# Linear attention in one pass: first q ahead of first v, filling matmuls behind the second head's transposes, v in whole rows for four of six buffers

## The chip, the cores and the metric

The kernel runs on one core of a Trainium2 chip. A core has TensorE (PE: matrix products, which take 128x128 weights, loaded by PEld, and stream columns past them), VectorE (DVE), ScalarE (ACT), GpSimd (POOL) and SyncE (SP), which here only issues transfers. PE writes to PSUM, eight banks of 512 fp32 columns on 128 partitions; everything else is kept in SBUF. Sixteen DMA engines move data between SBUF and the memory outside. The metric is the device time of one execution in microseconds (us).

## The reference

For each of 32 heads with 2048 rows of q, k and v, 128 wide, in bf16:

```python
phi_q = jnp.where(q > 0, q + 1, jnp.exp(q)) + 1e-6
phi_k = jnp.where(k > 0, k + 1, jnp.exp(k)) + 1e-6
kv  = jnp.einsum("bhsd,bhse->bhde", phi_k, v)      # 128 x 128 for each head
z   = jnp.einsum("bhsd->bhd", phi_k)               # sum of phi_k over the rows
num = jnp.einsum("bhqd,bhde->bhqe", phi_q, kv)
den = jnp.einsum("bhqd,bhd->bhq", phi_q, z)[..., None] + 1e-6
return num / den
```

The kernel writes phi(x) as min(exp(x), 1) + 1e-6 plus max(x, 0), and for most tiles never adds the two halves: PE accumulates both products.

## The kernel before, in words

A head is 16 tiles of 128 rows. Each head's q, k and v come in as one transfer of 512 KB, 4 KB on each partition, into one of six input buffers (NBI, head number modulo six, `bi`); results leave from ten output buffers.

For head h, in order of the data:

- ACT makes `ek_sb` = exp(k) (line 329); DVE turns it into `emk_sb` (min with 1, plus epsilon, line 335); POOL makes `rk_sb` = max(k, 0) (line 331) and, for tiles 1 to 5 (ADD), adds the two halves (line 340).
- PE multiplies phi(k) by v into the one bank `kvz_ps` (lines 356 and 359): two products for each of the eleven tiles of SPLIT, one for each of the five of ADD, 27 in all, which I call kv. The sum z needs a further column of ones beside v. Where a tile of v lies next to a gap of ones in SBUF, the product takes 129 columns at once. Everywhere else a matmul of a single column follows, with the same weights (`mm_held`, recorded under line 278).
- PE transposes q, 16 times, into `x_ps` (line 374); ACT makes exp of both halves (`eq_sb`, line 385) and max(q, 0) of the second (line 388), DVE that of the first (line 391); DVE makes `emq_sb` (line 394).
- ACT and DVE copy kv and z to `kvs_sb` (lines 364 and 366). PE multiplies phi(q) by it into the five banks `o_ps` (lines 412 and 418): the numerators and, as a 129th column, the denominators. DVE adds epsilon, takes reciprocals and multiplies (lines 457, 461, 433, 439). In the last heads ACT takes a part of that.

v lies in SBUF as two groups of eight tiles, with 32 columns of ones ahead of, between and behind them; one POOL memset of all three gaps in all six buffers makes these (line 274). So tiles 0, 7, 8 and 15 have ones at their side, and a row of v arrives as two pieces of 2 KB. Head 0 is another matter: its v goes to a buffer of its own, `v0_sb`, without gaps.

The order on each engine is a sort by a key given to every step (`Plan.add`), roughly the head's number plus a fraction; semaphore waits follow from what a step reads and writes. On PE a round is: numerators of head h, then transposes and kv of head h+2; ahead of the first round stand transposes and kv of heads 0 and 1. Heads in the middle are a loop of four turns of six heads on PE. On SP the stores have keys that grow faster than the heads', so that they fall behind the loads.

Until the first q is there, PE runs twelve products of zeros, 128x512 each, into the banks `o_ps` 2 to 4 (`warm`, lines 289 and 278, called on line 297). The first loads are issued in this order. On SP: k of head 0, q of head 0, k of head 1, q of head 1, v of head 1, and so on. On ACT's own queue: v of head 0 (line 316).

Of the kernel before, what the change touches and what calls it, by code (L numbers as in the profile page):

```python
# [11 lines left out]
def _ap(base: bass.AP, elem_offset: int, dims):  # L12
    return bass.AP(base.tensor, base.offset + elem_offset, [list(base.ap[0])] + [list(d) for d in dims])
# [162 lines left out]
def bass_standalone__linear_attn_elu__prompt_kernel(  # L176
# [6 lines left out]
    B, H, S, D = q.shape  # L183
    assert D == P and S == 16 * P
    NT = 16
# [3 lines left out]
    NBI = 6  # L189
# [6 lines left out]
    SPLIT = tuple(j for j in range(NT) if j not in ADD)  # L196
    GAP, GRP = 32, 8 * D
    VW = 2 * GRP + 3 * GAP

# [13 lines left out]
    LOOP, TURNS = 3, 4  # L215
# [6 lines left out]
    with ExitStack() as es:  # L222
# [4 lines left out]
        v_sb = sb("v_sb", [P, NBI, VW], bf16)  # L227
        q_sb = sb("q_sb", [P, NBI, NT * D], bf16)
        v0_sb = sb("v0_sb", [P, NT * D], bf16)
# [29 lines left out]
        pl = Plan()  # L259

        def rows(x, h):
            return x[h].rearrange("(p j) d -> p (j d)", j=NT)
# [8 lines left out]
        pl.add("pool", -7, lambda g: g.memset(ones_sb[:], 1.0), writes=[("ones",)])  # L271

        vfull = v_sb[:, :, :]
        pl.add("pool", -7, lambda g: g.memset(_ap(vfull, 0, [[VW, NBI], [GAP + GRP, 3], [1, GAP]]), 1.0), writes=[("vones",)])

        def mm_held(pe, out, lhsT, rhs, start, stop):

# [5 lines left out]
        def warm(n):  # L283

            def f(pe):
# [8 lines left out]

        pl.add("act", -9, lambda a: a.activation(rden_sb[:, 0, 0:1], warm_sb[:, 0:1], ACT.Exp), reads=[("warm",)],
               writes=[("rden", 0, 0)])
        pl.add("pe", -9, warm(12), reads=[("warm",)], writes=[("banko", 2), ("banko", 3), ("banko", 4)])

# [6 lines left out]
        for h in range(NH):  # L307
# [4 lines left out]

            def load(name, buf, src, key, h=h, bi=bi):
                dst, rws = buf[:, bi], rows(src, h)
                if h == 0 and name == "v":
                    pl.add("act", -8, lambda a: a.dma_start(v0_sb[:], rws), writes=[(name, bi)], dma=("x", 0))
                    return
                if name == "v":
                    dst = _ap(vfull, bi * VW + GAP, [[GAP + GRP, 2], [1, GRP]])
                    rws = rws.rearrange("p (a b) -> p a b", b=GRP)  # L320
                pl.add("sp", key, lambda sp: sp.dma_start(dst, rws), writes=[(name, bi)], dma=(name, bi))  # L321
# [22 lines left out]
            def kv(pe, tiles, srcs, h=h, bi=bi, b3=b3):  # L344
                for j in tiles:
                    for src in srcs:
                        first, fin = (j == SPLIT[0] and src is emk_sb), j == ADD[-1]
                        w = src[:, b3, j * D:(j + 1) * D]
                        c = GAP + (GAP + GRP) * (j // 8) + D * (j % 8)
                        l, r = (1, 0) if j % 8 == 0 else (0, 1) if j % 8 == 7 else (0, 0)  # L350
                        z = NC * r if h == 0 else 0
                        if h == 0:
                            rhs, l, r = v0_sb[:, j * D:(j + 1) * D], 0, 0
                        else:
                            rhs = v_sb[:, bi, c - l:c + D + r]
                        last = pe.matmul(kvz_ps[:, 1 - l:NC + r], lhsT=w, rhs=rhs, start=first, stop=fin,  # L356
                                         skip_group_check=True)
                        if not l + r:
                            last = mm_held(pe, kvz_ps[:, z:z + 1], w, ones_sb[:, 0:1], False, fin)
                return last  # L360
            pl.add("pe", at("kv", -1.2), lambda pe, kv=kv: kv(pe, SPLIT, (emk_sb, rk_sb)),
                   reads=[("emk", b3), ("rk", b3), ("v", bi), ("ones",), ("vones",)], writes=[("bankkv",)])
            pl.add("pe", at("kv", -1.2), lambda pe, kv=kv: kv(pe, ADD, (rk_sb,)), reads=[("phik", b3), ("v", bi)], writes=[("bankkv",)])
            pl.add("act", at("kvs", -0.95), lambda a, b3=b3: a.activation(kvs_sb[:, b3, 1:], kvz_ps[:, 1:NC], ACT.Copy),
                   reads=[("bankkv",)], writes=[("kvs", b3)])
# [123 lines left out]
            for n, (t0, t1) in enumerate(PIECES.get(h, ((0, NT),))):  # L489
                store(t0, t1, late + 0.01 * n, bo if n == 0 else NBO + EXTRA[h] + n - 1)  # L490

        pl.emit(block, sems, dma_sem, ("pe", 1 + LOOP * 9, NBI * 9, TURNS))


# [26 lines left out]
```

## Time and profile before

| What | us |
| --- | --- |
| median of three runs | 170.31 |
| lowest and highest of them | 170.14, 170.51 |
| the profiled execution | 170.35 |
| its span, first to last instruction | 168.5 |

| Engine | busy us | share of the span |
| --- | --- | --- |
| PE (matmuls) | 159.2 | 94% |
| PEld (loads of weights) | 151.7 | 90% |
| ACT | 158.1 | 94% |
| DVE | 150.3 | 89% |
| POOL | 105.5 | 63% |
| transfers of q1, the main queue | | 98.7% of 16 engines' span |

The profile is one execution. A group's busy time is the union of its instructions; matmuls overlap, so that a record of 0.22 us may be followed by the next one after 0.06 us: what a step costs on PE is read from start to start. The idle time before an instruction is shown with what ended it. The page's strips cut the span into 40 slices of 4.2 us, with a digit for tenths of the slice; PEclk is the granted clock of TensorE in the same tenths.

### The profile page before, as it was taken

The numbers are of one execution on the slowest core, as the hardware profiler recorded it, in microseconds if no ns is written. First come the engines' busy times: TensorE is split into PE (matmuls) and PEld (weight loads), VectorE is DVE, ScalarE is ACT, GpSimd is POOL, SyncE is SP. The second block draws the span as 40 slices with busy tenths as digits, with TensorE's granted clock in tenths as the row PEclk, the third lists the DMA queues.
The fourth block names the chain that finished last, engine by engine and source line by source line (L and its number), as shares of the span: only waits on it lengthen the run. The fifth ranks groups of instructions, "written<-read, shape, count | busy, mean of one in ns | idle before, by whom it ended". The sixth has DMA issues, their size and how long they took to land.

```text
span 168.5 us, 6577 instructions
## 1 busy us (share of the span) xinstructions
PE 159.2 (94%) x3092; PEld 151.7 (90%) x2401; DVE 150.3 (89%) x293; ACT 158.1 (94%) x180; POOL 105.5 (63%) x72
## 2 busy tenths in 40 slices
PE   7959999999999999999999999999999999999960
PEld 0459999999999999999999999999999999999940
DVE  0164799999999999999999999999999999999890
ACT  4699999999999999999999999999999999996980
POOL 3837746666777666666777666666777666666200
PEclk9995999999999999999999999999999999999997
DMA  5999999999999999999999999999999999999984
GB/s 207 408 415 410 411 409 407 409 406 414 412 408 410 416 415 415 419 414 416 415 415 416 417 410 420 414 419 415 415 414 417 418 414 417 413 413 416 391 327 163
DMA packets 22852, 67.33 MB, mean 400 GB/s; under 512 B 2100, under 2 KB 2612, under 8 KB 22836
## 3 DMA queue, kind: packets, MB, share of 16 engines
q1 hardware_dynamic: 22692, 66.59, 98.7%
q10 hardware_dynamic: 144, 0.52, 0.8%
q8 instruction: 10, 0.16, 0.4%
q14 instruction: 6, 0.05, 0.1%
HBM read 50.33 MB, written 16.78 MB: 398 GB/s over the span
## 4 chain that ended last, share of the span: by engine, by line
PE 88%; DMA 3%; DVE 3%; ACT 3%; issue 0%; SPq 0%
PE kvz_ps L356 36%; PE o_ps L412 32%; PE x_ps L374 16%; DMA q_sb<-in_q_dram 3%; DVE o_sb L439 1%; PE o_ps L278 1%; ACT eq_sb L385 1%; PE kvz_ps L278 1%; PE o_ps L418 1%; ACT ek_sb L329 1%; ACT rq_sb L388 1%; DVE emk_sb L335 0%; DVE rden_sb L461 0%; DVE den_sb L457 0%; SPq L321 0%
## 5 line engine op out<-in xcount | busy, mean ns | idle before, releaser
L340 POOL TENSOR_TENSOR rk_sb<-rk_sb,emk_sb 128x640 bf16<-128x640 bf16 x32 | 44.7, 1396 | 48.1 <-DVE emq_sb L394 43.8
L356 PE MATMUL kvz_ps<-v_sb,rk_sb 128*128 128x128 bf16 (+1 forms) x512 | 68.4, 219 | 0.0
L439 DVE TENSOR_TENSOR o_sb<-o_ps,rden_sb 128x768 bf16<-128x768 f32 (+2 forms) x63 | 68.0, 1119 | 0.1
L385 ACT ACTIVATE eq_sb<-x_ps 128x1024 bf16<-128x1024 bf16 x64 | 62.0, 1022 | 3.3 <-PE x_ps L374 3.3
L329 ACT ACTIVATE ek_sb<-k_sb 128x2048 bf16<-128x2048 bf16 x32 | 61.9, 1933 | 1.7 <-DMA k_sb<-in_k_dram 1.7
L331 POOL TENSOR_SCALAR rk_sb<-k_sb 128x2048 bf16<-128x2048 bf16 x32 | 60.6, 1894 | 2.7 <-DMA k_sb<-in_k_dram 2.0
L412 PE MATMUL o_ps<-kvs_sb,emq_sb 128*128 128x129 bf16 x474 | 60.7, 220 | 0.3 <-DVE o_sb L439 0.3
L412 PE MATMUL o_ps<-kvs_sb,rq_sb 128*128 128x129 bf16 x474 | 60.7, 220 | 0.0
L356 PE MATMUL kvz_ps<-v_sb,emk_sb 128*128 128x128 bf16 (+1 forms) x352 | 55.8, 220 | 2.1 <-DVE kvs_sb L366 2.1
L278 PE MATMUL kvz_ps<-ones_sb,rk_sb 128*128 128x1 bf16 x388 | 53.6, 167 | 0.0
L356 PEld LDWEIGHTS kvz_ps<-v_sb,rk_sb 128*128 128x128 bf16 x512 | 47.5, 98 | 1.5
L412 PEld LDWEIGHTS o_ps<-kvs_sb,rq_sb 128*128 128x128 bf16 x474 | 46.3, 98 | 0.0
L412 PEld LDWEIGHTS o_ps<-kvs_sb,emq_sb 128*128 128x128 bf16 x474 | 45.6, 98 | 0.6 <-DVE o_sb L439 0.4
L278 PE MATMUL kvz_ps<-ones_sb,emk_sb 128*128 128x1 bf16 x228 | 37.8, 167 | 0.0
L356 PEld LDWEIGHTS kvz_ps<-v_sb,emk_sb 128*128 128x128 bf16 x352 | 34.0, 98 | 2.3 <-issue 2.3
L374 PEld LDWEIGHTS x_ps<-ident,q_sb 128*128 128x128 bf16 x512 | 29.9, 98 | 5.5 <-DMA q_sb<-in_q_dram 5.5
L374 PE MATMUL x_ps<-ident,q_sb 128*128 128x128 bf16 x512 | 33.8, 219 | 0.3 <-DMA q_sb<-in_q_dram 0.3
L388 ACT ACTIVATE rq_sb<-x_ps 128x1024 bf16<-128x1024 bf16 x32 | 33.1, 1035 | 0.0
L335 DVE TENSOR_SCALAR emk_sb<-ek_sb 128x2048 bf16<-128x2048 bf16 x32 | 21.9, 684 | 8.3 <-ACT ek_sb L329 8.3
L391 DVE TENSOR_SCALAR rq_sb<-x_ps 128x1024 bf16<-128x1024 bf16 x32 | 21.8, 681 | 2.0 <-ACT eq_sb L385 2.0
L394 DVE TENSOR_SCALAR emq_sb<-eq_sb 128x2048 bf16<-128x2048 bf16 x32 | 22.7, 708 | 0.4 <-ACT eq_sb L385 0.4
L433 DVE TENSOR_TENSOR o_sb<-o_ps,rden_sb 128x128 bf16<-128x128 f32 x31 | 9.0, 291 | 1.0
(39 smaller groups left out, 80.2 us busy)
## 6 DMA issues: line engine op xcount, KB each, us to landing
k_sb<-in_k_dram SPq DMA_DIRECT2D x32, 512.0 KB, 13.2
q_sb<-in_q_dram SPq DMA_DIRECT2D x32, 512.0 KB, 13.1
v_sb<-in_v_dram SPq DMA_DIRECT2D x31, 512.0 KB, 13.6
out_dram<-o_sb SPq DMA_DIRECT2D x29, 512.0 KB, 13.4
out_dram<-o_sb SPq DMA_DIRECT2D x2, 320.0 KB, 9.2
out_dram<-o_sb SPq DMA_DIRECT2D x3, 192.0 KB, 3.6
v_sb<-in_v_dram ACTq DMA_DIRECT2D x1, 512.0 KB, 4.2
out_dram<-o_sb SPq DMA_DIRECT2D x1, 184.0 KB
```

The source lines that it names most:

```text
L278: return pe.add_instruction(mybir.InstMatmult(name=nc.get_next_instruction_name(), engine=mybir.EngineType.PE, ldweights=False, ins=[pe.lo ...
L329: lambda a, bi=bi, b2=b2: a.activation(ek_sb[:, b2, :], k_sb[:, bi, :], ACT.Exp),
L331: pl.add("pool", h, lambda g, bi=bi, b3=b3: g.tensor_scalar(rk_sb[:, b3, :], k_sb[:, bi, :], BIG, 0.0, op0=ALU.min, op1=ALU.max), reads=[( ...
L335: lambda d, b2=b2, b3=b3: d.tensor_scalar(emk_sb[:, b3, :], ek_sb[:, b2, :], 1.0, EPS, op0=ALU.min, op1=ALU.add),
L340: pl.add("pool", h + 0.5, lambda g, added=added: g.tensor_tensor(out=added(rk_sb), in0=added(rk_sb), in1=added(emk_sb), op=ALU.add), reads ...
L356: last = pe.matmul(kvz_ps[:, 1 - l:NC + r], lhsT=w, rhs=rhs, start=first, stop=fin, skip_group_check=True)
L374: last = pe.transpose(xT_ps[:, j * P:(j + 1) * P], q_sb[:, bi, j * P:(j + 1) * P], ident[:])
L385: lambda a, b2=b2, c=cols(half): a.activation(eq_sb[:, b2, c], xT_ps[:, c], ACT.Exp),
L388: lambda a, b3=b3, c=cols(1): a.activation(rq_sb[:, b3, c], xT_ps[:, c], ACT.Relu),
L394: lambda d, b2=b2, b3=b3: d.tensor_scalar(emq_sb[:, b3, :], eq_sb[:, b2, :], 1.0, EPS, op0=ALU.min, op1=ALU.add),
L412: last = pe.matmul(o_ap, lhsT=x[:, b3, t * P:(t + 1) * P], rhs=kvs_sb[:, b3, :], start=first, stop=not first)
L439: return lambda d: d.tensor_tensor(out=o_sb[:, bo, t0:t1, :].rearrange("p (a b) d -> p a b d", b=n), in0=_ap(nfull(b), 512 * b + NC * (t0 ...
```

## The change

There are three edits.

1. The first q is issued from ACT's queue, where the first v was. The first v takes the next key on SP, second there, behind the first k, and lands in `v0_sb` as before.
2. The warming products ahead of the first transposes are eleven, not twelve. Five more, of the same form, are placed on PE between the second head's transposes and its kv (key -0.22).
3. For buffers 1, 2, 4 and 5 (`WHOLE`) v lies as one group of sixteen tiles with ones ahead and behind, and its row arrives as one piece of 4 KB. There only tiles 0 and 15 have ones at their side; tiles 7 and 8 get the one-column matmul. Buffers 0 and 3 stay as they were. The ones are set by three POOL memsets. Of heads 1 to 31, 21 use a buffer with whole rows.

PE's loop begins one step later in its list, since there is one step more ahead of it.

```diff
+    WHOLE = (1, 2, 4, 5)
...
-        pl.add("pool", -7, lambda g: g.memset(_ap(vfull, 0, [[VW, NBI], [GAP + GRP, 3], [1, GAP]]), 1.0), writes=[("vones",)])
+        for n, (c, dims) in enumerate(((0, [[VW, NBI]]), (GAP + GRP, [[3 * VW, 2], [GAP + GRP, 2]]),
+                                       (VW + GAP + 2 * GRP, [[3 * VW, 2], [VW, 2]]))):
+            pl.add("pool", -7, lambda g, c=c, dims=dims: g.memset(_ap(vfull, c, dims + [[1, GAP]]), 1.0), writes=[("vones", n)])
...
-        pl.add("pe", -9, warm(12), reads=[("warm",)], writes=[("banko", 2), ("banko", 3), ("banko", 4)])
+        pl.add("pe", -9, warm(11), reads=[("warm",)], writes=[("banko", 2), ("banko", 3), ("banko", 4)])
+
+        pl.add("pe", -0.22, warm(5), reads=[("warm",)], writes=[("banko", 2), ("banko", 3), ("banko", 4)])
...
+                if h == 0 and name == "q":
+                    pl.add("act", -8, lambda a: a.dma_start(dst, rws), writes=[(name, bi)], dma=("x", 0))
+                    return
                 if h == 0 and name == "v":
-                    pl.add("act", -8, lambda a: a.dma_start(v0_sb[:], rws), writes=[(name, bi)], dma=("x", 0))
-                    return
-                if name == "v":
+                    dst = v0_sb[:]
+                elif name == "v" and bi in WHOLE:
+                    dst = v_sb[:, bi, GAP:GAP + 2 * GRP]
+                elif name == "v":
                     dst = _ap(vfull, bi * VW + GAP, [[GAP + GRP, 2], [1, GRP]])
                     rws = rws.rearrange("p (a b) -> p a b", b=GRP)
...
-                        c = GAP + (GAP + GRP) * (j // 8) + D * (j % 8)
-                        l, r = (1, 0) if j % 8 == 0 else (0, 1) if j % 8 == 7 else (0, 0)
+                        n = NT if bi in WHOLE else NT // 2
+                        c = GAP * (1 + j // n) + D * j
+                        l, r = (1, 0) if j % n == 0 else (0, 1) if j % n == n - 1 else (0, 0)
...
-        pl.emit(block, sems, dma_sem, ("pe", 1 + LOOP * 9, NBI * 9, TURNS))
+        pl.emit(block, sems, dma_sem, ("pe", 2 + LOOP * 9, NBI * 9, TURNS))
```

More of the change, by code (lines that the diff above doesn't have):

```diff
@@ L361, in bass_standalone__linear_attn_elu__prompt_kernel @@
             pl.add("pe", at("kv", -1.2), lambda pe, kv=kv: kv(pe, SPLIT, (emk_sb, rk_sb)),
-                   reads=[("emk", b3), ("rk", b3), ("v", bi), ("ones",), ("vones",)], writes=[("bankkv",)])
+                   reads=[("emk", b3), ("rk", b3), ("v", bi), ("ones",)] + [("vones", n) for n in range(3)],
+                   writes=[("bankkv",)])
             pl.add("pe", at("kv", -1.2), lambda pe, kv=kv: kv(pe, ADD, (rk_sb,)), reads=[("phik", b3), ("v", bi)], writes=[("bankkv",)])
```

## The prediction

> **What bounds the kernel now.** I read the page from the top: engines, clock and DMA over time, and the chain that ended last.
>
> ```profile
> PE 159.2 (94%) x3092; PEld 151.7 (90%) x2401; DVE 150.3 (89%) x293; ACT 158.1 (94%) x180; POOL 105.5 (63%) x72
> ...
> PEclk9995999999999999999999999999999999999997
> DMA  5999999999999999999999999999999999999984
> ...
> PE 88%; DMA 3%; DVE 3%; ACT 3%; issue 0%; SPq 0%
> ```
>
> Four resources look full: PE, ACT, DVE and the DMA engines. The chain says which of them the end hangs on: 88% of it is PE. The clock has one digit of 5, in the fourth slice. The list of waits shows when PE stood still:
>
> ```profile
> PEld x_ps L374 <- DMA q_sb<-in_q_dram: 5.5, 1, 5.5
> ...
> PE kvz_ps L356 <- DVE kvs_sb L366: 2.1, 1, 2.1
> ...
> PE x_ps L412 <- DVE den_sb L457: 0.3, 1, 0.3
> ...
> PE o_ps L412 <- DVE o_sb L439: 0.3, 1, 0.3
> ```
>
> Columns are total, times, longest. After the first q and one wait of 2.1 us PE waits 0.6 us in all, at the end. So from the second head on every microsecond on PE is one of the kernel's, and the start decides how late that stream begins. The timeline has its landmarks (start, duration, idle before):
>
> ```profile
> 5.66 0.63 PE L278 MATMUL o_ps<-warm_sb 128*128 128x512 bf16 x1
> ...
> 12.93 0.22 PE L356 MATMUL kvz_ps<-v_sb,emk_sb 128*128 128x129 bf16 x1 [2.12 <-DVE kvs_sb L366]
> ...
> 16.22 0.27 PE L412 MATMUL o_ps<-kvs_sb,emq_sb 128*128 128x129 bf16 x1
> ...
> 18.16 1.06 PE L374 MATMUL x_ps<-ident,q_sb 128*128 128x128 bf16 x16
> 19.05 0.22 PE L356 MATMUL kvz_ps<-v_sb,emk_sb 128*128 128x129 bf16 x1
> ...
> 47.45 0.22 PE L356 MATMUL kvz_ps<-v_sb,emk_sb 128*128 128x129 bf16 x1
> ...
> 49.46 0.22 PE L412 MATMUL o_ps<-kvs_sb,emq_sb 128*128 128x129 bf16 x1
> ...
> 51.30 1.06 PE L374 MATMUL x_ps<-ident,q_sb 128*128 128x128 bf16 x16
> ```
>
> A steady head takes 2.01 us for kv (47.45 to 49.46) and 1.84 for the numerators, 3.85 together. The same two of the start (kv of head 1, numerators of head 0) take 18.16 - 12.93 = 5.23: the slow clock costs 1.38 us. The table by stage, in stretches of 3.41 us, shows how it came (columns: length, then busy time and count of PE, PEld, DVE, ACT, POOL; clock, DMA share, GB/s):
>
> ```profile
> 9.68:13.08 3.40, 1.28 (x25) 1.11 (x20) 1.74 (x4) 3.40 (x5) 0.60 (x2) 1.00 1.04 427
> 13.09:16.50 3.41, 3.41 (x50) 3.27 (x29) 1.43 (x2) 3.41 (x4) 2.70 (x2) 0.50 1.04 408
> ...
> 159.87:163.27 3.40, 2.76 (x45) 2.28 (x40) 3.06 (x11) 2.94 (x10) 0.00 (x0) 1.00 0.83 335
> ```
>
> After a stretch with PE 1.28 busy (38%) the clock is half for exactly one stretch; after one with 2.76 (81%), at the tail, it stayed full.
>
> **The change part by part: v in whole rows.** 21 heads (remainder 1, 2, 4 or 5 by six) now have ones beside the first and last tile only. Tiles 7 and 8, each with two weights, lose their 129th column and need a one-column matmul of their own: 4 more per head, 84 in all. Their price stands in the trace twice, because head 0 has all 27 products in that form (54 matmuls) and a steady head 19 of 27 (46):
>
> ```profile
> 7.52:9.73 2.21, 2.21 (x54) 2.18 (x27) 0.00 (x0) 0.00 (x0) 1.00 1.02 406
> 47.45:49.46 2.01, 2.01 (x46) 1.96 (x27) 0.00 (x0) 0.00 (x0) 1.00 1.05 419
> ```
>
> Eight more cost 0.20 us, 0.025 each; 84 x 0.025 = 2.1 us, all on PE and so on the path. The rows' two decimals leave 0.19 to 0.21, or 2.0 to 2.2 us. I take 2.1.
>
> What it gives is fewer packets: 21 x 128 = 2,688 of 22,692. Its worth comes from a stage where a quarter of the bytes are in half rows beside one of 4 KB stores only (packets, MB, share of 16 engines; the whole span, then stretches of 80 and of 7 us):
>
> ```profile
> q1 hardware_dynamic: 22692, 66.59, 98.7%
> ...
> q1 hardware_dynamic: 11210, 32.93, 102.7%
> ...
> q1 hardware_dynamic: 788, 2.88, 101.7%
> ```
>
> Per engine 32.93 / (1.027 x 80 x 16) is 25.05 GB/s, 2.88 / (1.017 x 7 x 16) is 25.28: at most 0.9% if all v were whole, two thirds of that here, about 1 us of the 166 that 98.7% of the span are. PE waits for no load after the first q, so I book nothing for it before the tail. At the tail (same columns as above):
>
> ```profile
> 164.00:165.00 1.00, 0.00 (x0) 0.00 (x0) 0.69 (x1) 0.61 (x3) 0.00 (x0) 1.00 0.62 236
> ```
>
> The engines are no longer full (0.62) while the last stores go out, so these wait for compute more than for a queue. A full queue would owe the gain its 1 us, an idle one nothing; with 0.38 idle I allow 0 to 0.3 and take 0.
>
> **First q ahead of first v.** The first q is issued from ACT's queue, where v was, and v takes q's place on SP's, second there; k of head 1 and all behind it keep their places. Chain of waits and issue rows:
>
> ```profile
> 1.18 5.39 DMA q_sb<-in_q_dram
> ...
> 6.61 0.64 PE x_ps L374 x8
> ...
> 7.27 1.94 ACT eq_sb L385 x2
> 9.21 0.92 ACT rq_sb L388
> 10.13 1.80 ACT ek_sb L329
> ...
> 11.95 0.69 DVE emk_sb L335
> ```
>
> ```profile
> 5.23 1.06 PE L278 MATMUL o_ps<-warm_sb 128*128 128x512 bf16 x2
> ...
> 0.97 0.37 ACTq L316 DMA_DIRECT2D v_sb<-in_v_dram  x1
> 3.96 1.91 ACT L329 ACTIVATE ek_sb<-k_sb 128x2048 bf16<-128x2048 bf16 x1 [1.73 <-DMA k_sb<-in_k_dram]
> ```
>
> ```profile
> v_sb<-in_v_dram SPq DMA_DIRECT2D x31, 512.0 KB, 13.6
> ...
> v_sb<-in_v_dram ACTq DMA_DIRECT2D x1, 512.0 KB, 4.2
> ```
>
> In v's place q lands at 0.97 + 4.2 = 5.2 instead of 6.57. The twelfth warming matmul, begun at 5.66, is dropped, so the transposes begin at 5.66. Eight of them and the hand-over took 0.66 us (6.61 to 7.27): ACT's first eq could begin at 6.3. But the warming matmuls still ran at 0.43 us each (two begin at 5.23 and 5.66), twice what 512 columns take in a steady head, though the clock's digits show 9 there; if the clock is half for the first eight transposes, about 0.44 more, 6.75. ACT's ek ends at 5.87 and does not hold it. So eq comes 0.5 to 0.95 us earlier, and from there ACT is without a gap to ek of head 1, whose emk releases kv of head 1: I take 0.65, kv at 12.28. The first v lands about 6.6 and its kv follows the transposes at about 6.7, so nothing waits there; if v were late, 2.5 us of PE idling before 12.28 cover it.
>
> **Five filling matmuls.** 128x512 each, 1.1 us at full clock (a steady 128 columns take 0.056: sixteen transposes from 18.16 to 19.05) and 2.1 at half. They stand after the second head's transposes, which end at about 10.1 (their second half waits for ACT's rq), and ahead of kv at 12.28: the idle 2.1 us covers either; were it gone they would cost 1.1. They wait for nothing and write banks which head 0's numerators overwrite later on the same engine. With them the stretch from 9.68 holds about 0.4 of transposes, 1.1 of filling and 0.8 of kv: 2.3 of 3.4, 68%, between the two rows above and nearer the 81% that kept the clock. I take it that the clock stays: -1.38. Ends: 0 and -1.38.
>
> [...]
>
> **What is late next.** If both gains come, PE is 0.65 + 1.38 - 0.1 = 1.93 us ahead at head 2's transposes (16.23) and wants kv of head 2 at 17.12. It needs DVE:
>
> ```profile
> 16.66 0.69 DVE L335 TENSOR_SCALAR emk_sb<-ek_sb 128x2048 bf16<-128x2048 bf16 x1 [1.92 <-ACT ek_sb L329]
> 18.36 0.18 DVE L457 TENSOR_SCALAR den_sb<-o_ps 128x20 f32<-128x20 f32 x1 [1.01 <-PE o_ps L412]
> ```
>
> Without den's wait of 1.01, and 0.65 earlier, DVE's emk ends at 16.70. In head 1 kv followed the end of emk (12.64) by 0.29, the small kvs between them; here den, 0.1, comes too: about 17.1, just in time. The loads lose slack too: v of head 28 is issued at 126.26 and takes 13.6, landing at 139.9, 2.2 us ahead of its kv at 142.11; the lead left by then is 1.9 - 17 x 0.1 = 0.2.
>
> ```profile
> 126.26 0.59 SPq L321 DMA_DIRECT2D v_sb<-in_v_dram  x1
> ...
> 142.11 0.22 PE L356 MATMUL kvz_ps<-v_sb,emk_sb 128*128 128x129 bf16 x1
> ```
>
> POOL's three small memsets in place of one lie before its first data and cost nothing.
>
> **Sum.** -0.65 - 1.38 + 2.1 = +0.07 us. The profiled execution took 170.35 us, 0.04 over the median of the three runs, 170.31: 170.4 on either.
>
> **The rivals.**
> (1) The clock drops all the same. For it: 68% is untested, and transposes may count differently from products. Against it: the 81% row. It decides once the stretch from 9.68 falls below the unknown mark between 38% and 81%. Then -0.65 + 2.1 = +1.45: 171.8, slower.
> (2) The start gains more and the tail shortens. q is there at 5.2 and eq moves by 0.95, the stores drain 0.3 sooner: -0.95 - 1.38 + 2.0 - 0.3 = -0.6: 169.7, faster. Against it: the cold warming matmuls.
> (3) The lead isn't usable: DVE holds kv of head 2 or loads hold PE in the middle, 0.5 us back: 170.9.
>
> **How the numbers follow.** My forecast has 0.55, its own range is 169.9 to 170.9; (1) 0.23, (2) 0.14, (3) 0.08. A measurement tells 0.2%, 0.34 us, from no change. Of the forecast's 0.55, about 0.13 falls below 169.97, 0.25 within and 0.17 above 170.65. Faster: 0.13 + 0.14 = 0.27; same 0.25; slower 0.17 + 0.23 + 0.08 = 0.48. The range 169.6 to 172.0 takes in (1) and (2) and leaves out their far sides.
>
> **What would show it.** First transposes near 5.7 and kv of head 1 near 12.3; no clock of 0.50 behind 13.09; kv of a head in whole rows 2.11 us and of the others 2.01; packets down by 2,688; PE without a wait from kv of head 2 on. A digit of 5 in the clock, a PE wait on DVE near 17, or waits on loads late in the run would make me wrong.

## The result, and the profile after

The changed kernel takes 169.63 us (median of 7 runs, 169.49 to 170.01) against 170.31 us before; the ratio is 0.9966, 95% interval 0.9957 to 0.9975. It is a third of a per cent faster. The forecast was 170.4 us; the result lies at the lower edge of the wide range (169.6 to 172.0) and outside the forecast's own range of 169.9 to 170.9 us. The profiled execution took 169.56 us, with a span of 167.7 us, 0.8 us less than before.

From the page of the changed kernel: span, engines, granted clock, DMA engines' busy share and GB/s in 40 slices, main queue, chain.

```profile
span 167.7 us, 6668 instructions
...
PE 160.3 (96%) x3180; PEld 152.9 (91%) x2402; DVE 149.6 (89%) x293; ACT 158.8 (95%) x180; POOL 105.9 (63%) x74
...
PEclk9999999999999999999999999999999999999997
DMA  5999999999999999999999999999999999999984
GB/s 207 409 420 419 412 415 414 378 394 416 410 422 410 416 419 420 420 411 418 421 414 421 418 416 417 421 418 414 420 421 417 419 419 418 412 416 416 400 336 172
...
q1 hardware_dynamic: 20004, 66.59, 98.5%
...
PE 91%; DVE 3%; ACT 3%; issue 0%
```

The digit 5 in the fourth slice of the clock is gone, the packets are 2,688 fewer, and by the chain PE still carries the end, more than before (91% against 88%). That last reading is the trap of this case, as the experiments show.

The timeline of the changed kernel at the start (start, duration, idle before):

```profile
5.37 1.06 PE L386 MATMUL x_ps<-ident,q_sb 128*128 128x128 bf16 x16
6.73 0.22 PE L367 MATMUL kvz_ps<-v_sb,emk_sb 128*128 128x128 bf16 x1 [0.30 <-DMA v_sb<-in_v_dram]
...
6.02 1.94 ACT L397 ACTIVATE eq_sb<-x_ps 128x1024 bf16<-128x1024 bf16 x2 [0.16 <-PE x_ps L386]
...
9.20 1.07 PE L386 MATMUL x_ps<-ident,q_sb 128*128 128x128 bf16 x16
10.11 0.38 PE L293 MATMUL o_ps<-warm_sb 128*128 128x512 bf16 x1
10.32 1.03 PE L282 MATMUL o_ps<-warm_sb 128*128 128x512 bf16 x4
11.68 0.22 PE L367 MATMUL kvz_ps<-v_sb,emk_sb 128*128 128x129 bf16 x1 [0.33 <-DVE kvs_sb L378]
...
15.60 1.06 PE L386 MATMUL x_ps<-ident,q_sb 128*128 128x128 bf16 x16
16.50 0.22 PE L367 MATMUL kvz_ps<-v_sb,emk_sb 128*128 128x129 bf16 x1
```

ACT's first eq begins at 6.02, 1.25 us earlier than the 7.27 before; kv of head 1 at 11.68, also 1.25 earlier. The transposes of head 2 begin at 15.60 in place of 18.16: PE is 2.56 us ahead there. By stretches (length, busy time and count of PE, PEld, DVE, ACT, POOL; clock, DMA share, GB/s), the two around the filling, and then kv of head 2 (whole rows) and of head 3 (half rows):

```profile
8.48:11.89 3.41, 2.95 (x42) 1.63 (x27) 1.15 (x4) 3.41 (x5) 2.30 (x2) 1.00 1.03 420
11.89:15.30 3.41, 3.41 (x79) 3.40 (x52) 1.37 (x2) 3.41 (x4) 2.70 (x2) 1.00 1.03 420
...
16.50:18.61 2.11, 2.11 (x54) 2.08 (x29) 2.08 (x3) 2.11 (x3) 2.11 (x2) 1.00 1.04 405
21.34:23.35 2.01, 2.01 (x49) 1.96 (x28) 2.01 (x3) 2.01 (x3) 2.01 (x2) 1.00 1.02 410
```

With the filling the stretch holds 2.95 of 3.41 us of PE work (86%), and the clock stays. A head in whole rows takes 0.10 us more. The lead of 2.56 us melts at that rate: DVE's last denominator (`den`, the last step that waits for PE) starts at 162.68 in place of 163.26, 0.58 us earlier. After the warming, the list of PE's waits shows 0.3 us each for `kvs_sb` and for v at the start, nothing in between, and the two at the end that were there before:

```profile
PE kvz_ps L367 <- DVE kvs_sb L378: 0.3, 1, 0.3
PE x_ps L424 <- DVE den_sb L469: 0.3, 1, 0.3
PE kvz_ps L367 <- DMA v_sb<-in_v_dram: 0.3, 1, 0.3
PE o_ps L424 <- DVE o_sb L451: 0.3, 1, 0.3
```

So far all fits a kernel bound by PE: -1.25 - 1.4 + 2.04 is -0.6, and the span fell by 0.8. The runs below say that this is not why it fell.

### The profile page after: what moved, and what is told of

Its sections match the earlier page's. It is cut to its first block, busy times and chain, and to the rows that moved or that the text cites. A ratio compares the mean times of both kernels' runs of the same rounds, so it can differ in the third digit from the quotient of the medians.

```text
span 167.7 us, 6668 instructions
## 1 busy us (share of the span) xinstructions
PE 160.3 (96%) x3180; PEld 152.9 (91%) x2402; DVE 149.6 (89%) x293; ACT 158.8 (95%) x180; POOL 105.9 (63%) x74
## 4 chain that ended last, share of the span: by engine, by line
PE 91%; DVE 3%; ACT 3%; issue 0%
PE kvz_ps L367 37%; PE o_ps L424 32%; PE x_ps L386 16%; PE o_ps L282 4%; DVE o_sb L451 1%; PE kvz_ps L282 1%; ACT eq_sb L397 1%; PE o_ps L430 1%; ACT ek_sb L339 1%; ACT rq_sb L400 1%; DVE emk_sb L345 0%; DVE rden_sb L473 0%; PE o_ps L293 0%; DVE den_sb L469 0%; DVE o_sb L445 0%
## 5 line engine op out<-in xcount | busy, mean ns | idle before, releaser
L367 PE MATMUL kvz_ps<-v_sb,rk_sb 128*128 128x128 bf16 (+1 forms) x512 | 69.2, 217 | 0.0
L397 ACT ACTIVATE eq_sb<-x_ps 128x1024 bf16<-128x1024 bf16 x64 | 63.7, 1075 | 2.1 <-PE x_ps L386 1.9
L339 ACT ACTIVATE ek_sb<-k_sb 128x2048 bf16<-128x2048 bf16 x32 | 63.6, 1988 | 1.7 <-DMA k_sb<-in_k_dram 1.7
L282 PE MATMUL kvz_ps<-ones_sb,rk_sb 128*128 128x1 bf16 x430 | 59.9, 165 | 0.0
L367 PE MATMUL kvz_ps<-v_sb,emk_sb 128*128 128x128 bf16 (+1 forms) x352 | 56.9, 218 | 0.6 <-DVE kvs_sb L378 0.3
L367 PEld LDWEIGHTS kvz_ps<-v_sb,rk_sb 128*128 128x128 bf16 x512 | 46.7, 96 | 1.1
L282 PE MATMUL kvz_ps<-ones_sb,emk_sb 128*128 128x1 bf16 x270 | 44.3, 165 | 0.0
L400 ACT ACTIVATE rq_sb<-x_ps 128x1024 bf16<-128x1024 bf16 x32 | 34.9, 1090 | 0.0
L406 DVE TENSOR_SCALAR emq_sb<-eq_sb 128x2048 bf16<-128x2048 bf16 x32 | 22.1, 689 | 0.4 <-ACT eq_sb L397 0.4
L376 ACT ACTIVATE kvs_sb<-kvz_ps 128x128 bf16<-128x128 f32 x32 | 11.5, 358 | 0.0
```

The lines of the kernel that those rows point to most:

```text
L282: return pe.add_instruction(mybir.InstMatmult(name=nc.get_next_instruction_name(), engine=mybir.EngineType.PE, ldweights=False, ins=[pe.lo ...
L339: lambda a, bi=bi, b2=b2: a.activation(ek_sb[:, b2, :], k_sb[:, bi, :], ACT.Exp),
L397: lambda a, b2=b2, c=cols(half): a.activation(eq_sb[:, b2, c], xT_ps[:, c], ACT.Exp),
L400: lambda a, b3=b3, c=cols(1): a.activation(rq_sb[:, b3, c], xT_ps[:, c], ACT.Relu),
L406: lambda d, b2=b2, b3=b3: d.tensor_scalar(emq_sb[:, b3, :], eq_sb[:, b2, :], 1.0, EPS, op0=ALU.min, op1=ALU.add),
```

## The experiments

Two theories were set against each other. By the first, which is the prediction's, the end follows PE: each microsecond gained ahead of the last denominator is one of the kernel's. By the second, the end is the later of two things: the last denominator and what has to follow it, or a floor that the DMA engines set, whatever PE does.

In the tables "last den" is the start of DVE's last `den`, "last landing" the moment at which the last store's data has landed (from the trace's completion events), both in us from the span's start in the profiled execution; "spans" is the median over the runs. The device time is the span and about 1.85 us more; in some runs of several kernels (the filling alone, the two whole buffers and the shortened compute among them) it was 2.2 to 3.5 us more, which no trace explains, and so spans are compared there.

### The three edits in all eight combinations

Only the first q ahead of the first v, out of the kernel before:

```diff
-                if h == 0 and name == "v":
-                    pl.add("act", -8, lambda a: a.dma_start(v0_sb[:], rws), writes=[(name, bi)], dma=("x", 0))
+                if h == 0 and name == "q":
+                    pl.add("act", -8, lambda a: a.dma_start(dst, rws), writes=[(name, bi)], dma=("x", 0))
                     return
-                if name == "v":
+                if h == 0 and name == "v":
+                    dst = v0_sb[:]
+                elif name == "v":
```

> The first edit alone (twelve warming matmuls, no filling, v in half rows). Theory A, the forecast's mechanism with its own size of 0.65 us: the clock still drops once, time 170.31 - 0.65 = 169.7. Theory B, the start gains what the changed kernel's trace shows from the first eq on (7.27 to 6.02): with the twelfth warming matmul still there up to 0.4 less, so about 0.85 to 1.25 us, 169.1 to 169.5. In both the kv of head 1 runs at half clock if the gap ahead of it still throttles.

Only the filling matmuls:

```diff
-        pl.add("pe", -9, warm(12), reads=[("warm",)], writes=[("banko", 2), ("banko", 3), ("banko", 4)])
+        pl.add("pe", -9, warm(11), reads=[("warm",)], writes=[("banko", 2), ("banko", 3), ("banko", 4)])
+        pl.add("pe", -0.22, warm(5), reads=[("warm",)], writes=[("banko", 2), ("banko", 3), ("banko", 4)])
```

> The second edit alone (eleven warming matmuls, five filling ones behind the second head's transposes, first q where it was, v in half rows). If the drop of the clock cost 1.38 us and the filling removes it: 170.31 - 1.38 = 168.9, and no stretch at 0.50 ahead of the end. If the drop had another cause, or its loss was made up elsewhere: 170.3.

Both of these, v in half rows everywhere (both diffs above together):

> The first two edits without whole rows. Theory B (every microsecond on PE counts): 169.63 less the 84 one-column matmuls of the changed kernel, 21 x 0.097 = 2.04 us, plus what whole rows give the tail, so 167.6 to 167.8; PE without waits. Rival (the loads could not follow such a lead: v of head 28 had 2.2 us of slack in the kernel before, and the lead is 2.6): PE waits 0.4 us or more for loads, 168.0 to 168.4. Rival (whole rows are needed by the lead and pay for themselves): 169.6 or more.

Only the whole rows (the third edit of the change alone; first v on ACT's queue, twelve warming matmuls, no filling):

> The third edit alone. If the one-column matmuls cost what kv shows in the changed kernel (2.11 instead of 2.01 for 21 heads) and nothing covers them: 170.31 + 2.04 = 172.3, or 172.1 if the tail gets 0.2 back. If whole rows pay for themselves through faster loads or stores: 170.3 or less.

The changed kernel without the filling:

```diff
-        pl.add("pe", -0.22, warm(5), reads=[("warm",)], writes=[("banko", 2), ("banko", 3), ("banko", 4)])
...
-        pl.emit(block, sems, dma_sem, ("pe", 2 + LOOP * 9, NBI * 9, TURNS))
+        pl.emit(block, sems, dma_sem, ("pe", 1 + LOOP * 9, NBI * 9, TURNS))
```

> The changed kernel without the five filling matmuls. If the gap of 1.9 us that then stands ahead of kv of head 1 throttles the clock as the 2.1 us one did, PE loses 1.3 us and, as compute sets the end with whole rows, 170.7 to 170.9, with a stretch of 3.41 us at 0.50 near 10 to 17 us. If the earlier q alone keeps the clock up: 169.6 and no such stretch.

The changed kernel with the first v on ACT's queue again:

```diff
-                if h == 0 and name == "q":
-                    pl.add("act", -8, lambda a: a.dma_start(dst, rws), writes=[(name, bi)], dma=("x", 0))
-                    return
                 if h == 0 and name == "v":
-                    dst = v0_sb[:]
-                elif name == "v" and bi in WHOLE:
+                    pl.add("act", -8, lambda a: a.dma_start(v0_sb[:], rws), writes=[(name, bi)], dma=("x", 0))
+                    return
+                if name == "v" and bi in WHOLE:
```

> The filling and the whole rows, without the earlier q (the missing one of the eight combinations). Floor theory (the end is the later of PE's end + 3.84 us and what the slowest DMA engines leave, 167.2 us in whole rows): the last den stands 0.72 us behind the changed kernel's 162.68 us, as it did between the runs with whole rows alone (165.42) and with whole rows and the q (164.70), so 163.40, and 163.40 + 3.84 = 167.24 us: the two ends meet, 169.6 to 169.9 us, without the spread of 1.4 us that the runs without filling showed. PE theory (each microsecond on PE counts): 169.63 + 0.72 = 170.35 us.

Measured (medians; ratio to the kernel before with its 95% interval):

| first q | filling | whole rows | us | ratio | spans | last den | last landing |
| --- | --- | --- | --- | --- | --- | --- | --- |
| no | no | no | 170.3 | 1 | 168.4 | 163.26 | 168.02 |
| yes | no | no | 170.15 | 0.9994 [0.9985, 1.0003] | 168.3 | 161.30 | 167.80 |
| no | yes | no | 170.53 | 1.0010 [1.0001, 1.0019] | 168.3 | 162.24 | 167.84 |
| yes | yes | no | 170.18 | 1.0004 [0.9991, 1.0017] | 168.3 | 161.28 | 167.85 |
| no | no | yes | 171.64 | 1.0060 [1.0037, 1.0082] | 169.7 to 170.0 or 168.3 to 168.5 | 165.42 | 169.26 |
| yes | no | yes | 170.11 | 0.9998 [0.9977, 1.0018] | 168.4 to 169.3 or 167.5 to 167.8 | 164.70 | 168.53 |
| no | yes | yes | 170.04 | 0.9986 [0.9977, 0.9995] | 168.2 | 164.15 | 167.99 |
| yes | yes | yes | 169.63 | 0.9966 [0.9957, 0.9975] | 167.8 | 162.68 | 167.23 |

The first four rows decide against the prediction's theory: q alone, and q with the filling, bring the last denominator 2.0 us forward, and the last data lands 0.2 us earlier; none of the times that were expected of an end that follows PE (169.1 to 169.7, 168.9, 167.6 to 167.8 us) came. DVE's last `den` in the kernels with q alone and with both:

```profile
161.30 0.17 DVE L459 TENSOR_SCALAR den_sb<-o_ps 128x12 f32<-128x12 f32 x1 [0.20 <-PE o_ps L414]
```

```profile
161.28 0.17 DVE L460 TENSOR_SCALAR den_sb<-o_ps 128x12 f32<-128x12 f32 x1 [0.20 <-PE o_ps L415]
```

The stretches at the end of the second of these kernels show what goes on after it (same columns as above):

```profile
164.00:165.00 1.00, 0.00 (x0) 0.00 (x0) 0.00 (x0) 0.00 (x0) 0.00 (x0) 1.00 0.78 290
165.00:166.00 1.00, 0.00 (x0) 0.00 (x0) 0.00 (x0) 0.00 (x0) 0.00 (x0) 0.82 0.30 116
166.00:167.00 1.00, 0.00 (x0) 0.00 (x0) 0.00 (x0) 0.00 (x0) 0.00 (x0) 0.50 0.19 69
167.00:168.00 1.00, 0.00 (x0) 0.00 (x0) 0.00 (x0) 0.00 (x0) 0.00 (x0) 0.50 0.05 18
```

No engine of the core works any more, and yet transfers go on for nearly four microseconds, from 165 us on at a share of 0.30, then 0.19, then 0.05: on average that is some five, three and one of sixteen engines still working. A share below one is thus not spare room for a late store here; it is many engines that are done and a few that are not, as the completion events of one store show further below.

In these two kernels the lead also met the loads, earlier in the run. It was 2.3 us until head 26. By the completion events, v of heads 27 and 28 lands at 135.00 and 140.04 us in the second of them, their kv start at 135.22 and 140.13, and 0.3 us of the lead is lost there (0.4 with q alone). The prediction had put the landing of v of head 28 at 139.9 us.

The other side of the second theory is in the last four rows. With whole rows alone, with q, and with the filling, the last landing is 3.84, 3.83 and 3.84 us behind the last `den` (169.26 - 165.42, 168.53 - 164.70, 167.99 - 164.15). There the end does follow PE. (With filling and whole rows the last `den` came 0.75 us later than expected, 164.15 against 163.40, but the sum with 3.84 holds.) In the changed kernel the distance is 4.55 us, in those with half rows 4.8 to 6.6: there it doesn't.

The filling, too, reads differently by its company. In half rows it is worth at most 0.1 us of span. In whole rows it decides between two times that one kernel takes: without it, and with the old order of loads, 9 of 12 executions had a mean granted clock of 0.982 to 0.986 and spans of 169.7 to 170.0 us, the other three 0.992 or 0.993 and 168.3 to 168.5. With the first q ahead, five of twelve had 0.982 to 0.984 and 168.4 to 169.3 us, seven 0.990 or more and 167.5 to 167.8 us. The profiled execution of that kernel is one of the five; its stretches:

```profile
9.89:13.30 3.41, 1.48 (x33) 1.32 (x20) 2.30 (x4) 3.41 (x5) 1.31 (x2) 1.00 1.02 419
13.30:16.72 3.42, 3.42 (x48) 3.32 (x30) 1.42 (x2) 3.42 (x5) 2.21 (x2) 0.50 1.03 418
```

and the wait of PE ahead of kv of head 1, which the filling covers in the changed kernel:

```profile
PE kvz_ps L366 <- DVE kvs_sb L377: 1.9, 1, 1.9
```

PE busy for 1.48 us of 3.41 (43%) was followed by one stretch at half clock. It began 6.82 us after the clock had gone full (6.48 to 13.30); before, and with whole rows alone, it began 6.83 us after (6.26 to 13.09, 6.64 to 13.47), and all three last 3.41 or 3.42 us. The half clock at the tail begins 160.43 us after that moment, in the kernel before as in the changed one: 47 times 3.413, as 6.83 is twice that. So the stretches are counted here from the moment at which the clock went full. Whether a stretch falls on the gap is chance: the clock went full at 5.07, 6.26, 6.48 and 6.64 us in four of the profiles (changed kernel, before, no filling, whole rows alone), and anywhere from 4.28 to 6.72 us in all of them. In the kernel before the drop seems to cost little: of 70 executions beside these runs, the 35 with the lower mean clock have a median span of 168.5 us and the others 168.3. That is a hint only, for the mean clock takes in the idle tail too (half from 166.69 us on in the profile); the filling alone, whose profile has no drop and whose span is 168.3 us, says the same. There the floor hides it. That the filling always keeps the clock isn't shown either: with the filling alone three of eleven executions have a mean clock of 0.977 or 0.978, less than any other run here, at the same spans, and none of the three was profiled.

The same chance moves the start of PE's stream. In the profile of the changed kernel with half rows (next section) the clock went full at 6.57 us, and the first transposes and ACT's first eq read:

```profile
5.66 1.50 PE L383 MATMUL x_ps<-ident,q_sb 128*128 128x128 bf16 x16
...
6.75 1.94 ACT L394 ACTIVATE eq_sb<-x_ps 128x1024 bf16<-128x1024 bf16 x2 [0.86 <-PE x_ps L383]
```

From transposes to eq it is 1.09 us there, in the changed kernel 0.65. So it went, to 0.02 us, in three more profiles with the first q and eleven warming matmuls in which the clock went full at 6.58 to 6.72 us; their last `den` lies at 163.3, while those of the same matmuls with a full clock by 5.2 us have 162.7 to 162.8. Last `den`s of single profiles thus differ by up to 0.7 us without an edit.

### The rows alone

The changed kernel with the same work on PE (84 more one-column matmuls, the two other edits), but with v in half rows everywhere:

```diff
-                elif name == "v" and bi in WHOLE:
-                    dst = v_sb[:, bi, GAP:GAP + 2 * GRP]
...
-                        c = GAP * (1 + j // n) + D * j
+                        c = GAP + (GAP + GRP) * (j // 8) + D * (j % 8)
```

> The changed kernel with the same matmuls on PE (84 one-column ones more), but v of every head in two half rows, as before. Theory D (the end hangs on the DMA engines that are last to finish, with half rows not before about 167.8 us of the span whatever PE does): compute ends where it does in the changed kernel, last den at 162.7, but the last store lands at about 167.8: 170.15. Rival (the end follows compute, whole rows are worth only the tail's 0 to 0.3 us): 169.6 to 169.9.

170.32 us (170.13 to 170.67), ratio 1.0005 [0.9996, 1.0014], span 168.4; last landing 167.95. The last `den` was expected at 162.7, where the changed kernel has it, and came 0.73 us later, by the late clock just shown:

```profile
163.41 0.17 DVE L466 TENSOR_SCALAR den_sb<-o_ps 128x12 f32<-128x12 f32 x1 [0.20 <-PE o_ps L421]
```

This isn't what holds the end: 163.41 + 3.84 is 167.25, and the last landing is 0.7 us behind that. Against the changed kernel, whose code differs in the packets alone (and in POOL's memsets of the ones), the time is 0.7 us longer: all of the gain of the change vanishes with the whole rows.

Then the compute was made shorter. The one-column matmuls behind the products are left out for all heads but the first, so that the sum over the keys is incomplete and the denominators are others:

```diff
-                        if not l + r:
+                        if not l + r and h == 0:
```

> The changed kernel without the one-column matmuls behind the kv matmuls of all heads but the first: the sums z over the keys are then incomplete and the output is another. This takes some 23 x 31 = 713 matmuls of 0.025 us from PE, after which ScalarE (busy 158.8 us) sets the pace; the last den comes 1 us or more earlier than 162.68 us. The transfers are the same. Floor theory: the last store still lands at 167.2 us, 169.4 to 169.7 us. PE theory (the changed kernel ends by its compute): it falls by as much as the last den, to 168.6 us or less.

169.88 us (169.41 to 170.51), ratio 0.9976 [0.9964, 0.9988]; the median span is 167.6 us against 167.8. DVE's last `den` and the stretches at the end:

```profile
159.74 0.17 DVE L469 TENSOR_SCALAR den_sb<-o_ps 128x12 f32<-128x12 f32 x1 [0.20 <-PE o_ps L424]
```

```profile
162.00:163.00 1.00, 0.00 (x0) 0.00 (x0) 0.00 (x0) 0.00 (x0) 0.00 (x0) 0.50 1.01 389
163.00:164.00 1.00, 0.00 (x0) 0.00 (x0) 0.00 (x0) 0.00 (x0) 0.00 (x0) 0.50 0.76 288
164.00:165.00 1.00, 0.00 (x0) 0.00 (x0) 0.00 (x0) 0.00 (x0) 0.00 (x0) 0.50 0.42 157
165.00:166.00 1.00, 0.00 (x0) 0.00 (x0) 0.00 (x0) 0.00 (x0) 0.00 (x0) 0.50 0.21 79
166.00:167.00 1.00, 0.00 (x0) 0.00 (x0) 0.00 (x0) 0.00 (x0) 0.00 (x0) 0.50 0.09 32
```

The last denominator comes 2.94 us earlier than in the changed kernel (159.74 against 162.68), and the last data lands at 167.18 against 167.23 us. This is the floor with nothing in front of it: 167.2 us in whole rows, where half rows have 167.8 to 167.95. The changed kernel stands on its floor too.

Whole rows in two buffers (11 heads) in place of four:

```diff
-    WHOLE = (1, 2, 4, 5)
+    WHOLE = (1, 4)
...
-        for n, (c, dims) in enumerate(((0, [[VW, NBI]]), (GAP + GRP, [[3 * VW, 2], [GAP + GRP, 2]]),
-                                       (VW + GAP + 2 * GRP, [[3 * VW, 2], [VW, 2]]))):
+        for n, (c, dims) in enumerate(((0, [[VW, NBI]]), (VW + GAP + 2 * GRP, [[3 * VW, 2]]), (GAP + GRP, [[3 * VW, 2], [GAP + GRP, 2]]), (2 * VW + GAP + GRP, [[3 * VW, 2], [GAP + GRP, 2]]))):
```

> Whole rows in two of the six buffers (11 heads) in place of four (21 heads): 10 x 0.097 = 0.97 us less on PE, so the last den at 161.7 us, and 1,280 packets more than the changed kernel. Floor theory: the floor goes from 167.2 us to about half way to the half rows' 167.9, 167.5 us; 169.9 to 170.0 us, slower than the changed kernel by 0.3. PE theory: 169.63 - 0.97 = 168.7 us.

170.06 us (169.71 to 170.34), ratio 0.9985 [0.9976, 0.9994], span 167.9; last den 162.14, last landing 167.37, between the two floors. The last `den` is 0.5 us earlier than the changed kernel's (1.0 was expected), which brings nothing here either; the price of the 1,280 packets that came back is 0.1 us of span.

### Which engines make the floor

One store in the middle, that of head 14, is issued in three parts of 80, 46 and 2 rows in all kernels so far (`UNEVEN`). Six runs change this cut. Without it, in half rows (with the first two edits) and in whole rows (the changed kernel):

```diff
-    UNEVEN = {14: (80, 46, 2)}
+    UNEVEN = {}
```

> The first two edits without whole rows, and the store of head 14 in one piece of 128 rows instead of 80, 46 and 2. Theory D with the particular that the 46 and 2 rows go to few of the sixteen engines and make these the last: the last store lands earlier by about 0.5 to 1 us, 169.2 to 169.7, with compute as before it (last den at 161.3). If the late engines are late for another reason: 170.2 or, as all engines carry three rows more, 170.6.

> The changed kernel with the store of head 14 in one piece. Compute ends at 162.7 as before, and the last store is already near what compute allows (2.7 us after its issue, 2.0 where the queues are empty): theory D expects 0 to 0.6 us less, 169.0 to 169.6. Its rival (the split store helps): 169.9 or more.

170.68 us, 1.0044 [1.0025, 1.0063], and 169.99 us, 0.9986 [0.9977, 0.9995]: last landings 168.34 and 167.66 us, each 0.4 to 0.5 later than with the cut (167.85, 167.23). The first was expected to gain by 0.5 to 1 us or to lose, the second to gain by up to 0.6 or to lose: both lost. The last denominators are where they were (161.29, 162.71).

A second store cut in the same way:

```diff
-    UNEVEN = {14: (80, 46, 2)}
+    UNEVEN = {14: (80, 46, 2), 20: (80, 46, 2)}
```

> The changed kernel with head 20's store also cut into 80, 46 and 2 rows, as head 14's is: of sixteen engines most get three rows (0.16 us each) fewer, two get many more. Late-engine theory (a few engines that aren't those two finish last): the floor goes down by up to 0.48 us, to 166.75 us, and PE's end + 3.84 = 166.5 us is not yet reached: 169.2 us. Even-load theory (each engine is as full as the others, the two loaded ones become the last): their 20 rows more take 3.2 us, so 170.0 us or more.

172.72 us (172.65 to 172.83), 1.0142 [1.0127, 1.0156]. The trace's completion events tell why. A transfer in one piece has sixteen of them, which I read as one report of each of sixteen engines, and it counts as landed with the last. In the changed kernel's trace the 80 rows have sixteen as well. The 46 rows have one at 107.67 us and two at their end, 120.10 and 120.68, the 2 rows one at 108.82 and two at 120.29 and 120.86: two engines, by that reading. A 4 KB row takes an engine 0.159 us, the median of that trace's packets of this size. These are the reports for head 29's store, the last in one piece, in order of time, and the landing of the last store (us):

```
kernel                       ninth    last four of sixteen             last store
before                       162.31   164.24 164.53 165.06 165.43      168.02
changed                      161.82   164.03 164.07 164.61 164.65      167.23
changed, no cut              162.31   163.08 163.49 164.64 165.09      167.66
changed, two heads cut       162.21   163.45 164.15 167.14 167.76      170.39
cut 16, 42, 70               162.26   162.43 163.07 164.52 165.26      167.86
cut 32, 72, 24               162.39   162.85 163.33 163.53 165.59      168.13
cut 32, 95, 1                162.26   163.28 163.66 164.87 167.15      169.68
```

In the changed kernel four engines are 2.2 to 2.8 us behind the ninth. With a second cut two reports stand 3.1 us later (167.14 and 167.76) and two 0.5 us or so earlier (163.45 and 164.15); the events don't name engines, but one pairing fits both. By it two of the four are late because they carry the 46 rows, and two are late of themselves; these stand at 164.64 and 165.09 without a cut. If sixteen engines share 128 rows evenly, and 80 too, the cut takes three rows off these two (0.43 us, 167.66 to 167.23) and makes two others just as late.

Two cuts that, by a counting that I supposed, take rows off engines at the other end of the count:

```diff
-    UNEVEN = {14: (80, 46, 2)}
+    UNEVEN = {14: (16, 42, 70)}
```

> Head 14's store cut into 16, 42 and 70 rows in place of 80, 46 and 2. The run with two heads cut moved exactly two engines by 3.1 us, so 46 rows go to two engines; I suppose that 42 and 70 rows go to fourteen (3 and 5 each) and that engines are counted from the same end, so that two engines at the other end get 1 row in place of 8 and fourteen get 9. If the two engines that are late of themselves are those two: they come 7 x 0.15 = 1.05 us ahead of the uncut kernel's 167.66 us, at 166.6 us, and the last den + 3.84 = 166.5 us ends with them: 169.0 us. If they are among the fourteen: 167.66 + 0.15 = 167.8 us, 170.1 us.

```diff
-    UNEVEN = {14: (80, 46, 2)}
+    UNEVEN = {14: (32, 72, 24)}
```

> Head 14's store cut into 32, 72 and 24 rows: by the same supposition twelve engines get 10 rows and the four at the other end 2 in place of 8. If the late engines are among those four: 6 x 0.15 = 0.9 us ahead of the uncut kernel's 167.66 us, 166.8 us, so 169.2 us. If they are among the twelve: 167.66 + 0.3 = 168.0 us, 170.3 us.

170.18 us, 0.9995 [0.9986, 1.0003], and 170.38 us, 1.0006 [0.9997, 1.0015]; last landings 167.86 and 168.13. Both came out as expected of a latest engine that is not among those eased (167.8 and 168.0). In the second, only one engine is still far behind (165.59 us, the next 163.53): by the counting, the other one was eased.

Last, five engines loaded and eleven eased:

```diff
-    UNEVEN = {14: (80, 46, 2)}
+    UNEVEN = {14: (32, 95, 1)}
```

> Head 14's store cut into 32, 95 and 1 rows: by the counting that the last two runs fit, five engines get 21 or 22 rows in place of 8 (13 more, 1.95 us, less than the 2.2 us by which the late ones stand behind the median) and eleven get 2 (6 fewer, 0.9 us). If the latest engine is among the eleven: 167.66 - 0.9 = 166.8 us, a little over the last den + 3.84 = 166.5 us, so 169.1 to 169.3 us, faster than the changed kernel. If it is among the five: 167.66 + 1.95 = 169.6 us, 171.6 us.

172.13 us, 1.0108 [1.0091, 1.0125], last landing 169.68: the expected landing of the bad case (169.6; the device time set beside it, 171.6 us, should have been 171.9, with the 2.3 us that lie between the two in most runs). So by the counting supposed, the latest engine is among the third to the fifth, the second latest the thirteenth or fourteenth. How many engines carry 42, 70, 72, 24 or 95 rows, and which, is supposed, not read from a trace. Three landings within 0.2 us of what was worked out by that counting agree with it (167.86, 168.13 and 169.68 against 167.8, 168.0 and 169.6). Loading two engines alone, as the cut of 80, 46 and 2 does, is the one form here that lowers the floor. No version that was run has a shorter device time than the changed kernel.

Why those two engines are late was not settled. Each kernel's trace has eight to ten fetches of instructions of 16 KB, 0.9 to 1.6 us each, on a queue of their own (q8, which the page counts on the same sixteen engines); the last in the changed kernel starts at 162.3 us. That one isn't what sets the end: with the shortened compute the last fetch starts at 153.2 us and with the filling alone at 156.0, and their last data lands at 167.18 and 167.84, as in the changed kernel (167.23) and with q alone (167.80), whose last fetch starts at 163.3. Whether the earlier fetches make the two engines late stays open.

## Why the prediction was wrong

**Right.** The clock stays with the filling in the profile (86% of the stretch, 68% predicted). The one-column matmuls cost 0.10 us a head: kv takes 2.11 and 2.01 us, as said; 20 heads from head 2 on are the 2.0 us by which the lead shrank from 2.56 to 0.58. The 0.10 is for four of them, 25 ns each. The packets fell by 2,688. In the changed kernel no wait of PE on loads came up after the start (v of head 28 lands at 139.60 us, its kv starts at 141.34), and DVE kept up with kv of head 2: rival (3) did not occur there. In half rows its second half did, with 0.3 to 0.4 us.

**Mis-sized: the first q.** -0.65 was booked; in the profile of the changed kernel it was -1.25. The transposes began at 5.37, not 5.66, and at full speed: from their start to ACT's eq 0.65 us. In the four profiles with the late clock it was -0.52, with transposes at 5.66 and eq at 6.75, the very times that the prediction had worked out for a half clock. In between lie -0.75 and -0.87, with the clock full at 6.11 and 5.84 us (half rows without the cut store, two whole buffers). So the size of this term in an execution is chance, by when the clock goes full; the one figure booked followed one profile, while that moment lies anywhere from 4.28 to 6.72 us in the 17 kept. With the term of this profile, the sum would give -1.25 - 1.38 + 2.04, about -0.6 us, 169.8, close to the measurement. That agreement is a coincidence: the kernels with the first two edits, or with q alone, end PE's work 2.0 us earlier than the kernel before and take the same time within 0.1 us of span.

**The step that failed** is "So from the second head on every microsecond on PE is one of the kernel's", and with it "these wait for compute more than for a queue" and the whole rows booked at nothing. All three rest on PE's lack of waits and on the mean share of the DMA engines at the tail, 0.62. PE did run without a wait; but behind its end the last stores had to wait for engines that were behind with earlier ones (the last four reports for head 29's store are 1.9 to 3.1 us behind the ninth in the kernel before), and a mean over sixteen doesn't show a late one. In the kernel before, the last landing was 4.76 us behind the last `den` (168.02 - 163.26), where 3.84 would do. So of what the sum added up:

- The start's gains on PE (the first q and the clock) were worth 0.1 us of span, not 2.0, as long as v came in half rows. They pay for the whole rows' matmuls: without the first q the changed kernel ends by PE, at 170.04 us, and without the filling it does so in five executions of twelve.
- The whole rows were booked at 0 for the transfers. They lower the floor by 0.6 to 0.7 us (from 167.8 to 167.95 in half rows to 167.2), which is nearly the whole gain of 0.8 us in the last landing; the other 0.1 to 0.2 is what the start brought. "About 1 us of the 166" was the right order for the engines' work; it was dropped because PE waits for no load.
- The matmuls' 2.1 us were real on PE (2.0 us by the profiles) and cost nothing in the time, since PE had 0.9 us to spare before and the start gave it up to 2.6 more.

Of the rivals, (2) gave the right number, 169.7, by a sum on PE with the stores 0.3 us shorter; its mechanism is not what happened. (1), 171.8, is what whole rows cost when the clock does drop and q isn't moved: 171.64. A rival "the end is held by transfers already; PE's gains are lost and the packets count" was missing, and its price could have been worked out: 168.5 us of span less 0 to 1.

A part of the packets' worth was not seen. 2,688 rows at 0.7 us are less than the 1 us of the estimate. The stretches of the changed kernel around 33 us show one place where the engines ran below their pace, and SP, which issues all transfers but the first q, standing behind a q buffer that PE still read:

```profile
32.00:33.00 1.00, 1.00 (x28) 0.98 (x14) 1.00 (x1) 1.00 (x3) 1.00 (x1) 1.00 1.02 356
33.00:34.00 1.00, 1.00 (x24) 1.00 (x19) 1.00 (x3) 1.00 (x3) 0.46 (x1) 1.00 0.94 270
```

```profile
32.15 4.95 SPq L331 DMA_DIRECT2D q_sb<-in_q_dram  x1
```

At the usual 420 GB/s these two are short of 64 and 150 GB/s, half a microsecond in all. Before, the lowest stretch there had 377. Whether another order of issue would win this back was not tried.

**On the clock's drop.** Without the filling, a wait of 1.9 us of PE, in the kernel with whole rows and the first q, gave the half clock, as the wait of 2.1 us did before. How busy the stretch was fits every profile kept here: counted in stretches of 3.41 us from the moment at which the clock went full, in all 17, each stretch that was followed by the half clock has PE busy for 43% of it or less, at the gap or at the tail, and each that was followed by the full clock for 62% or more (the lowest is 2.13 of 3.42 us, from 159.80 with the filling alone). The stretch with the filling is 70 to 77% busy in the four profiles with the late clock, near the 68% of the prediction; with q alone, and no filling, a wait of 1.4 us fell across two stretches of 74% and 79%. What a stretch between 43% and 62% is followed by isn't shown.

## What to carry to other kernels

Before you count a gain on the busiest engine, find out what is between its last instruction and the last landing: put the distance from the last compute step to the last store's landing beside the shortest distance that any variant shows; what was more than that here (4.55 us and more against 3.84) was a floor by transfers, and gains on the engine were lost in it. A mean DMA share below one at the tail may be a few late engines rather than free ones (here 0.30, 0.19 and 0.05, with no engine of the core at work); look at how the reports of one store's sixteen engines spread. When a cheap saving on transfers costs an engine that has slack, make sure that the slack doesn't hang on chance, such as a clock that drops in some executions (here in nine of twelve with whole rows alone, in five of twelve with the first q as well).

## What was not expected of the hardware

- Two of sixteen engines were 2.3 and 2.8 us behind the ninth at the end of the run without a cut (164.64 and 165.09 against 162.31 us), and by the counting supposed they were the same ones in the cuts tried.
- A row of 4 KB in a store costs its engine about 0.15 us (its packet in the trace 0.159): a second cut moved two reports by 3.1 us, 21 rows more for each of two engines by the counting supposed, and three rows fewer, by the same, brought the end 0.43 us forward.
- A kernel that ends by PE and has no filling takes two times, 1.4 us apart with whole rows alone and 1.0 with the first q as well, by where, as far as the two profiles show, a stretch of 3.41 us, counted from the moment at which the clock went full, falls on a gap of PE of some 2 us.
- In some kernels the device time is 0.3 to 1.7 us longer than usual with the same span, in part of the runs; nothing in a trace of the core shows it.
